# Attention backward: fewer tiles of dS turned on TensorE, more dP tiles on GpSimd, and smaller pieces of the turned QKV weights

## The chip, the core and the metric

The kernel runs on one core of a Trainium2 chip. A core has five engines that work side by side and meet at semaphores: PE (TensorE, matrix products into PSUM), DVE (VectorE), ACT (ScalarE), POOL (GpSimd) and SP (SyncE, which here only issues DMAs). Sixteen DMA engines move the data. The metric is the device time of one launch in microseconds (us); lower is better. The kernel before takes 2510.57 us, the median of three runs (2510.35 to 2513.57).

## The reference

The program computes the output of one transformer block and the gradients of ten of its inputs. The sequence has S = 2048 rows of D = 512 values, there are 32 heads of width 16, and the MLP is 1792 wide. Cut to what matters:

```python
mod = (silu(c) @ w_mod).reshape(1, 6, 1, 512)      # sa, ca, ga, sb, cb, gb
h = layernorm(x) * (1 + ca) + sa
q, k, v = heads(h @ wqkv)                          # 32 heads, Dh = 16
p = softmax(q @ k.T * Dh ** -0.5)
x = x + ga * (merge(p @ v) @ wo)
h = layernorm(x) * (1 + cb) + sb
x = x + gb * (relu(h @ w1 + b1) ** 2 @ w2 + b2)
out, vjp = jax.vjp(block, x, wqkv, wo, w1, b1, w2, b2, c, w_mod)
return out, *vjp(grad_out)
```

The change lies in the backward of the softmax attention. For each head it needs the scores again, P = exp(scale q k^T) (the row sums have been worked into dO and the delta term before), dP = dO v^T - delta, dS = P * dP, and from these dV = P^T dO, dK = dS^T q and dQ = dS k.

## The kernel before, in words

The program is one chain of stages. From the start to about 980 us runs the attention forward, with the QKV projection and the MLP forward as filler; from there to about 1168 us the MLP backward; from about 1168 to 2385 us the attention backward (`attn_bwd`, L1431 on), which is what the change touches; and to 2509 us the weight gradients of QKV and `wo`, the input gradient and the modulation (`phase6`).

**Tiling of the attention backward.** The outer loops run over eight head groups `g` of four heads, and over two pairs `jp` of heads in each: 16 pairs in all. In a pair, `c` runs over four chunks of 512 query columns, and `ib0` over four **groups** of four key-side blocks of 128 rows. So a pair has 16 groups; the text numbers them m = 0 to 15 (L1586). A group is even or odd by m. A group has four steps `i`, a step has the two heads `a` of the pair.

**A step.** For each head PE makes a score tile `st` (L1601, 128x512 in PSUM) and, one step behind, the `dp` tile of the step before (L1522). These two use different halves of the array's rows. ACT takes `st` to `pu = exp(st)` (L1604). DVE takes `dp` and `pu` to `ds = dp * pu` (L1526, bf16 in SBUF). PSUM holds three `st` tiles (pool `p5st`) and three `dp` tiles (`p5dp`), so PE can be at most that far ahead of ACT and of DVE. PE also runs `kv` (L1459, four small matmuls side by side for dK and dV of a step, `kv_two`), and `dq` (L1484, four matmuls side by side for dQ).

**Turning dS.** `dq` needs dS transposed. The `ds` of a whole group (32 blocks of 128x128) is turned by one DMA on SP's queue (`dS`, L1543) into one of five buffers `dsT` (the fifth is a part of `keep`). In the even groups PE turns the four blocks of the first step's first head itself (`turn_ds`, L1550: four transposes at L1559 into a tile from the `st` pool, and one copy by ACT at L1560), so that group's DMA turns only 28 blocks. In the odd groups the DMA turns all 32. Two consecutive groups are put together: their eight `dq` calls are queued (`pendq`) when the second one's DMA is issued, and PE starts them two groups later, two calls in step 0 and two in step 2 of each group (L1614). The text calls two such groups, an even one and the odd one behind it, a **window**.

**Help from GpSimd.** In the odd groups (`off`, L1528), one of the eight dS tiles, that of step 1 and head 1, isn't made by DVE: ACT copies the `dp` tile to SBUF (`dP_pool`, L1534, into `junk6` or `csq` in turn) and POOL multiplies (L1535). In the odd groups the `kv` work is also spread differently: one step's `kv` after the first head and one at the end of the step, in place of two at the end.

**Loads.** The next pair's and next group's operands come in pieces: before each group POOL issues the piece that is due (L1586 to L1590), after a one-element copy `tick` (L1589) that reads a recent `ds` and so holds the issue back to its place. The pieces of a pair are evenly spaced over its 16 groups: 16 in most. In the first pair of the last head group (g = 7, jp = 0) there are 16 as well: four of `pair_pieces`, four of the QKV weights and eight of `WmT`, the turned QKV weights that `phase6` needs (`load_wmt`, 128 rows of 1536 bytes each). All engines keep the order in which the program is written here; nothing is reordered by a scheduler in this stage.

Every so often there is more: at the end of a chunk ACT takes dK and dV out of PSUM (`kvT`, L1462, four in a pair), and in groups 2, 3 and 7 of a pair the finished dK, dV and dQ of the pair before are turned on PE (`turn`, L1472 and L1500) and copied by ACT (L1476, L1502).

The lines that order it, from the functions printed below:

```python
        def off(c, ib):
            return (c * SC + ib // G) % 2 == 1
...
                            if i == 2:
                                turn_ds(dsg, grp, off(c, ib), end and m > 2)
```

Of the kernel before, what the change touches and what calls it, by code (L numbers as in the profile page):

```python
# [19 lines left out]
P = 128  # L20
# [15 lines left out]
class Background:  # L36
# [13 lines left out]
    def next(self):  # L50
        while self.gens:
            r = next(self.gens[0], None)
            if r is not None:
                if isinstance(r, tuple):
                    self.mark = r[0]
                    self.seen.add(r[0])
                return r
            self.gens.pop(0)
        return None
# [46 lines left out]
class K:  # L106
# [1277 lines left out]
    def load_wmt(self):  # L1384

        D, DT = self.D, self.DT
        self.WmT = self.wp.tile([P, DT, 3 * DT, P], BF16, name="WmT")
        return [(self.WmT[:, kt, n:n + 6].rearrange("p n k -> p (n k)"), self.WmT_d[kt, :, n * P:(n + 6) * P])
                for kt in range(DT) for n in range(0, 3 * DT, 6)]

    def load_group(self, g):

# [4 lines left out]
        if g < 2:  # L1397
            T, o = {}, 0
            for n, e in width.items():
                if g:  # L1400
                    T[n] = qp.tile([P, e], BF16, name=f"{n}g")[:]
                elif n == "K":
                    T[n] = self.keep[:, :e]
                else:
                    T[n] = self.q0[:, o:o + e]
                    o += e
            self.Tq[g] = T
        T, pieces = self.Tq[g % 2], []
        for n, (src, rows) in fm.items():
# [21 lines left out]
    def attn_bwd(self):  # L1431
# [8 lines left out]
        S, D, H, NQ, ST, SC = self.S, self.D, self.H, self.NQ, self.ST, self.SC  # L1440
        G = 4
# [8 lines left out]
        pend, pendq, turnq, two = [], [], [], []  # L1450
        own = dT_free[-1]

        def kv(u):
            (T, g, jp, c, ib, kvT, pu, ds) = u
            for j, (n, src) in enumerate((("Q", ds), ("dO", pu))):
                for a in range(2):
                    r = 64 * j + 32 * a
                    col = (2 * jp + a) * DH
                    nc.tensor.matmul(acckv[r:r + DH, :], lhsT=T[n][:, ib, col:col + DH], rhs=src[:, a, :],  # L1459
                                     start=(ib == 0), stop=(ib == ST - 1))  # L1460
            if ib == ST - 1:
                nc.scalar.activation(kvT[:, 512 * c:512 * (c + 1)], acckv[:], ACT.Copy, scale=kvs[:])  # L1462
# [42 lines left out]
        def kv_two(n=2):  # L1505
            for _ in range(n):
                u = pend.pop(0)
                kv(u)
                (T, g, jp, c, ib, kvT, pu, ds) = u
                if ib < ST - 1:  # L1510
                    continue
                if c % 2 and (g, jp) == (NQ - 1, 1):
                    turnq.append((g, jp, kvT, 4 * (c - 1)))
                elif c == SC - 1:
                    turnq.extend((g, jp, kvT, s0) for s0 in (0, ST // 2))

        def dP(u, a):

            (T, g, jp, c, ib, kvT, pu, dsg, i, grp) = u
            rd = slice(64 - 64 * jp, 128 - 64 * jp)  # L1520
            dp = dpp.tile([P, 512], F32, name="dp")
            nc.tensor.matmul(dp[:], lhsT=T["dOT"][rd, ib * P:(ib + 1) * P],  # L1522
                             rhs=masked["VT"][a][rd, 512 * c:512 * (c + 1)], start=True, stop=True)
            if a == 1 and i == 1 and off(c, ib):
                return dp
            nc.vector.tensor_tensor(dsg[:, i, a], dp[:], pu[:, a, :], ALU.mult)  # L1526

        def off(c, ib):  # L1528
            return (c * SC + ib // G) % 2 == 1

        def dP_pool(u, dp):
            (T, g, jp, c, ib, kvT, pu, dsg, i, grp) = u
            f = (self.junk6, self.csq)[(c * SC + ib // G) // 2 % 2]
            nc.scalar.copy(f[:], dp[:])  # L1534
            nc.gpsimd.tensor_tensor(dsg[:, i, 1], f[:], pu[:, 1, :], ALU.mult)  # L1535

# [13 lines left out]
        def turn_ds(dsg, grp, skip, late):  # L1550

            dsT = next(t for t in dT_free if not late or t is not own)
            dT_free[:] = [t for t in dT_free if t is not dsT]
            grp.extend((dsT, 0 if skip else 4))
            if skip:
                return
            tp = stp.tile([P, 4, P], BF16, name="st")
            for b in range(4):
                nc.tensor.transpose(tp[:, b, :], dsg[:, 0, 0, b * P:(b + 1) * P], self.ident[:])  # L1559
            nc.scalar.copy(dsT[:, 0:4 * P], tp[:].rearrange("p b k -> p (b k)"))  # L1560

        tick = self.tick
        T = self.T0
        last = None
        for g in range(NQ):
            for jp in range(2):
                if jp == 0:
                    if g + 1 < NQ:
                        Tn, later = self.load_group(g + 1)
                    else:  # L1570
                        Tn, later = None, self.wq_pieces(1) + self.load_wmt()
                    cut = len(later) // 2 if Tn else len(later)
                    pieces = self.pair_pieces(g, 1) + later[:cut]
                    later = later[cut:]
                elif g + 1 < NQ:
                    pieces = self.pair_pieces(g + 1, 0) + later
                else:
                    pieces = [(self.xhat1_6[:, st, :], self.xhat1_d.rearrange("(st p) d -> p st d", p=P)[:, st, :])
                              for st in range(ST)]
                kvT = kvp.tile([P, S], BF16, name="kvT")  # L1580
                end = (g, jp) == (NQ - 1, 1)
                total = len(pieces)
                for c in range(SC):
                    c0 = 512 * c
                    for ib0 in range(0, ST, G):
                        m = c * (ST // G) + ib0 // G  # L1586
                        while pieces and (total - len(pieces)) * SC * ST <= m * G * total:
                            if last:
                                nc.gpsimd.tensor_copy(tick[:], last[7][0:1, 0, 0, 0:1])  # L1589
                            nc.gpsimd.dma_start(*pieces.pop(0))  # L1590
                        dsg, grp = self.dsp.tile([P, G, 2, 512], BF16, name="ds"), []
                        for i in range(G):
                            ib = ib0 + i
                            q = slice(ib * P, (ib + 1) * P)
                            if turnq and i == 3 and m >= (7 if turnq[0][2] is None else 2):
                                turn(*turnq.pop(0))
                            pu = self.pup.tile([P, 2, 512], BF16, name="pu")
                            for a in range(2):
                                stt = stp.tile([P, 512], F32, name="st")
                                rs = slice(64 * jp, 64 * jp + 64)  # L1600
                                nc.tensor.matmul(stt[:], lhsT=T["QT"][rs, q], rhs=masked["KT"][a][rs, c0:c0 + 512],  # L1601
                                                 start=True, stop=True)
                                held = dP(last, a) if last else None
                                nc.scalar.activation(pu[:, a, :], stt[:], ACT.Exp, scale=self.scale)  # L1604
                                if held is not None:
                                    dP_pool(last, held)
                                if a == 0 and i % 2 == 1 and off(c, ib) and len(pend) >= 4:
                                    kv_two(1)
                            if last:
                                dS(last)  # L1610
                            last = (T, g, jp, c, ib, kvT, pu, dsg, i, grp)
                            if i % 2 == 1 and len(pend) >= 4:
                                kv_two(1 if off(c, ib) else 2)
                            elif i % 2 == 0 and len(pendq) > 2 * G:  # L1614
                                for _ in range(4 if end else 2):
                                    dq(pendq.pop(0))
                            if i == 2:
                                turn_ds(dsg, grp, off(c, ib), end and m > 2)
            T = Tn
        with tc.manual_schedule(engines=ALL):  # L1620
            for t in (2, 0):
# [337 lines left out]
```

## Time and profile before

| what | value |
|---|---|
| median of 3 runs | 2510.57 us (2510.35 to 2513.57) |
| the profiled execution's own time | 2511.14 us |
| its span, first to last instruction | 2509.0 us |
| mean granted TensorE clock | 0.997 of full speed |
| attention backward in the span | about 1168 to 2385 us |
| exps of it (L1604) | 2048, 128 in a pair of heads |
| dS tiles by DVE (L1526) / by POOL (L1535) | 1920 / 128 |
| transposes of dS by PE (L1559) / copies of them by ACT (L1560) | 512 / 128 |
| DMA transposes (L1543) | 256, half of 28 blocks and half of 32 |

The span is what the profile covers; the device time is 2.1 us longer, for what lies around it. A row of the profile names a line, an engine, an operation and the tiles it writes and reads (out<-in), then the number of instructions, the busy time and the mean length of one. The length of one is longer than its share of the time where instructions overlap in the engine's pipeline: what counts for the pace is the distance from one start to the next. A view of the time line merges instructions of the same kind that follow each other: start, length of the whole stretch, and their number behind an x.

### The profile page before, as it was taken

The page shows a single profiled execution, that of the slowest core. Times are in us where ns is not written, and L with a number is a line of the kernel's source. Part 1 is how long each engine was busy: PE and PEld are TensorE (multiplying, and loading weights), DVE is VectorE, ACT ScalarE, POOL GpSimd, SP SyncE. Part 2 cuts the span into 40 slices and gives each one's busy share as a digit, 9 for nine tenths or more (in the row PEclk, how much of TensorE's full clock was granted, in tenths as well). Part 3 has the DMA queues.
Part 4 walks back from the last instruction along what each step waited for, and adds up shares of the span by engine and source line. Part 5 has one row for each costly group of instructions (what it writes and reads, how often), then busy time and mean ns, then how long its engine had stood idle before and what let it go on. Part 6 is the DMA issues. An engine that isn't in the chain of part 4 may idle for free.

```text
span 2509.0 us, 68721 instructions
## 1 busy us (share of the span) xinstructions
PE 2438.6 (97%) x26695; PEld 1080.0 (43%) x26695; DVE 1709.6 (68%) x3519; ACT 2295.0 (91%) x3789; POOL 716.4 (29%) x1289
## 2 busy tenths in 40 slices
PE   8999999999999999999999999999999999999998
PEld 4555555555555554573333333333333333333343
DVE  6222322422332344677999999999999999999957
ACT  7999999999999997534999999999999999999935
POOL 2344531220131022245222222222222222222223
PEclk9999999999999999999999999999999999999999
DMA  4688661441243044598999999999999999999997
GB/s 166 133 180 208 170 121 50 129 100 39 99 115 90 23 131 138 122 199 214 236 215 227 224 221 228 223 222 221 229 222 222 230 223 222 225 226 232 233 191 208
DMA packets 1260526, 445.78 MB, mean 178 GB/s; under 512 B 1204052, under 2 KB 1228246, under 8 KB 1260198
## 3 DMA queue, kind: packets, MB, share of 16 engines
q1 hardware_dynamic: 1219654, 336.29, 70.7%
q0 software_dynamic: 38464, 104.04, 13.6%
q8 instruction: 209, 3.42, 0.6%
q10 hardware_dynamic: 2080, 1.05, 0.1%
q14 instruction: 119, 0.97, 0.1%
HBM read 75.83 MB, written 64.49 MB: 56 GB/s over the span
## 4 chain that ended last, share of the span: by engine, by line
PE 58%; ACT 27%; DMA 7%; issue 4%; DVE 3%; POOL 1%; SPq 0%; DVEq 0%; ACTq 0%; POOLq 0%
ACT pu L391 18%; PE st L1601 17%; PE acckv L1459 8%; PE st L388 8%; ACT pu L1604 7%; PE accq L1484 5%; DMA dsT<-ds 3%; PE accbank L322 3%; PE dps L1050 2%; PE pps L1237 2%; PE st L1559 1%; PE dp L1522 1%; PE dp L1652 1%; DVE ds L1526 1%; DMA keep<-ds 1%
## 5 line engine op out<-in xcount | busy, mean ns | idle before, releaser
L1526 DVE TENSOR_TENSOR ds<-dp,pu 128x512 bf16<-128x512 f32 x1920 | 1181.7, 684 | 25.1 <-PE dp L1522 19.1
L1604 ACT ACTIVATE pu<-st 128x512 bf16<-128x512 f32 x2048 | 1072.7, 661 | 30.1 <-PE st L1601 21.3
L391 ACT ACTIVATE pu<-st 128x1024 bf16<-128x1024 f32 x992 | 912.2, 1077 | 5.1 <-PE st L388 4.9
L388 PE MATMUL st<-QTm,KTq 128*128 128x512 bf16 x1984 | 588.4, 377 | 20.0 <-ACT pu L391 6.0
L322 PEld LDWEIGHTS <-pu 128*128 128x128 bf16 x8192 | 347.3, 96 | 236.3 <-issue 3.2
L1522 PE MATMUL dp<-kvm,q 64*128 64x512 bf16 x1024 | 364.1, 384 | 1.5 <-DVE ds L1526 0.7
L1522 PE MATMUL dp<-kvm,dOTg 64*128 64x512 bf16 x1024 | 361.8, 384 | 0.5 <-DVE ds L1526 0.4
L322 PE MATMUL accbank<-Vaug,pu 128*128 128x17 bf16 x8192 | 357.7, 171 | 1.2 <-ACT Vaug L522 0.9
L1601 PE MATMUL st<-kvm,q 64*128 64x512 bf16 x1024 | 351.6, 381 | 6.0 <-ACT pu L1604 0.2
L1601 PE MATMUL st<-kvm,QTg 64*128 64x512 bf16 x1024 | 350.6, 381 | 6.8
L388 PEld LDWEIGHTS <-KTq 128*128 128x128 bf16 x1984 | 188.2, 96 | 177.5 <-issue 125.6
L1535 POOL TENSOR_TENSOR ds<-junk,pu 128x512 bf16<-128x512 f32 x64 | 73.8, 1153 | 372.2 <-ACT junk L1534 302.4
L1459 PE MATMUL acckv<-ds,Qg 128*16 128x512 bf16 x1024 | 176.0, 382 | 0.2
L1459 PE MATMUL acckv<-pu,dOg 128*16 128x512 bf16 x1024 | 175.9, 382 | 0.0
L1459 PE MATMUL acckv<-ds,q 128*16 128x512 bf16 x1024 | 175.8, 382 | 0.0
L1459 PE MATMUL acckv<-pu,q 128*16 128x512 bf16 x1024 | 175.8, 382 | 0.0
L1535 POOL TENSOR_TENSOR ds<-csq,pu 128x512 bf16<-128x512 f32 x64 | 73.8, 1154 | 349.6 <-ACT csq L1534 271.5
L302 POOL DMA_DIRECT2D QTm<-QTq_d x124 | 63.8, 516 | 341.5 <-PE st L388 319.9
L1601 PEld LDWEIGHTS <-q 64*128 64x128 bf16 x1024 | 66.9, 94 | 159.6 <-issue 144.0
L1601 PEld LDWEIGHTS <-QTg 64*128 64x128 bf16 x1024 | 67.0, 94 | 158.2 <-issue 141.3
L329 DVE RECIPROCAL rl<-accbank 128x4 f32<-128x4 f32 x128 | 23.0, 179 | 159.0 <-PE accbank L322 158.8
L1522 PEld LDWEIGHTS <-q 64*128 64x128 bf16 x1024 | 89.8, 93 | 56.7 <-issue 50.4
(390 smaller groups left out, 3197.0 us busy)
## 6 DMA issues: line engine op xcount, KB each, us to landing
KTq<-KTq_d POOLq DMA_DIRECT2D x24, 512.0 KB, 3.8
duT_d<-auT POOLq DMA_DIRECT2D x3, 1792.0 KB, 7.6
aT_d<-rT POOLq DMA_DIRECT2D x3, 1792.0 KB, 11.0
KTq_d<-KTq SPq DMA_DIRECT2D x32, 128.0 KB, 2.1
QTq_d<-ev_fm SPq DMA_DIRECT2D x32, 128.0 KB, 4.3
ktm_d<-ev_tm POOLq DMA_DIRECT2D x32, 128.0 KB, 2.5
VTq_d<-vT POOLq DMA_DIRECT2D x4, 1024.0 KB, 6.2
dx<-dx_d SPq DMA_DIRECT2D x16, 256.0 KB, 5.3
```

Source lines behind the costliest of these rows:

```text
L302: nc.gpsimd.dma_start(QTm[j][32 * j:32 * j + 32, :], self.QTq_d[g, 32 * j:32 * j + 32, 512 * qc:512 * (qc + 1)])
L322: nc.tensor.matmul(acc[:, a, sub, :], lhsT=pu[:, a, sub * P:(sub + 1) * P], rhs=Vaug[:, kb, h, :], start=(kb == 0 and a == 0 and sub == 0) ...
L388: nc.tensor.matmul(stt[:, a, :], lhsT=KT[:, kb * P:(kb + 1) * P], rhs=QTm[2 * jp + a][:], start=True, stop=True)
L391: nc.scalar.activation(pu[:], stt[:], ACT.Exp, scale=self.scale)
L1050: nc.tensor.matmul(pt[:], lhsT=a[st], rhs=g_tm[:, st, :], start=(st == 0), stop=(st == ST - 1))
L1459: nc.tensor.matmul(acckv[r:r + DH, :], lhsT=T[n][:, ib, col:col + DH], rhs=src[:, a, :], start=(ib == 0), stop=(ib == ST - 1))
L1484: nc.tensor.matmul(accq[r:r + 32, o:o + 256], lhsT=T["K"][:, 4 * c + sub, col:col + 32], rhs=v[:, r // 32 % 2 * 2:r // 32 % 2 * 2 + 2, 4 * ...
L1522: nc.tensor.matmul(dp[:], lhsT=T["dOT"][rd, ib * P:(ib + 1) * P], rhs=masked["VT"][a][rd, 512 * c:512 * (c + 1)], start=True, stop=True)
L1526: nc.vector.tensor_tensor(dsg[:, i, a], dp[:], pu[:, a, :], ALU.mult)
L1535: nc.gpsimd.tensor_tensor(dsg[:, i, 1], f[:], pu[:, 1, :], ALU.mult)
L1601: nc.tensor.matmul(stt[:], lhsT=T["QT"][rs, q], rhs=masked["KT"][a][rs, c0:c0 + 512], start=True, stop=True)
L1604: nc.scalar.activation(pu[:, a, :], stt[:], ACT.Exp, scale=self.scale)
```

## The change

It has three parts. First, `turn_ds` is called with another rule, `no_turn`: PE turns its four blocks only in groups 0, 4, 8 and 12 of a pair. In groups 2, 6, 10 and 14 the transposes on PE and ACT's copy are gone, and the DMA turns 32 blocks there. Second, `off` is also true in groups 10 and 14, so that ten tiles of a pair go by ACT and POOL in place of eight; the rule for spreading `kv` keeps the old condition under the name `odd`. `dP_pool` takes `csq` in odd groups and `junk6` in even ones. Third, `WmT` is fetched in sixteen pieces of 128 rows of 768 bytes in place of eight of 1536 bytes, one in each of the first 14 pairs as the fifth piece of the pair (behind the four of `pair_pieces`), and two in the 15th, which is the first of the last head group and then has ten pieces in place of 16. Most pairs then have 17 pieces, and a new clause issues what is left before group 15.

```diff
-        return [(self.WmT[:, kt, n:n + 6].rearrange("p n k -> p (n k)"), self.WmT_d[kt, :, n * P:(n + 6) * P])
-                for kt in range(DT) for n in range(0, 3 * DT, 6)]
+        return [(self.WmT[:, kt, n:n + 3].rearrange("p n k -> p (n k)"), self.WmT_d[kt, :, n * P:(n + 3) * P])
+                for kt in range(DT) for n in range(0, 3 * DT, 3)]
...
+        def odd(c, ib):
+            return (c * SC + ib // G) % 2 == 1
+
+        def no_turn(c, ib):
+            return ib // G > 0
+
         def off(c, ib):
-            return (c * SC + ib // G) % 2 == 1
+            return odd(c, ib) or (c > 1 and ib // G == 2)
 
         def dP_pool(u, dp):
             (T, g, jp, c, ib, kvT, pu, dsg, i, grp) = u
-            f = (self.junk6, self.csq)[(c * SC + ib // G) // 2 % 2]
+            f = (self.junk6, self.csq)[(c * SC + ib // G) % 2]
...
+        wmt = self.load_wmt()
...
-                        Tn, later = None, self.wq_pieces(1) + self.load_wmt()
+                        Tn, later = None, self.wq_pieces(1) + wmt[2 * g + 1:]
                     cut = len(later) // 2 if Tn else len(later)
-                    pieces = self.pair_pieces(g, 1) + later[:cut]
-                    later = later[cut:]
+                    pieces = self.pair_pieces(g, 1) + wmt[2 * g:2 * g + 1] + later[:cut]
+                    later = wmt[2 * g + 1:2 * g + 2] + later[cut:]
...
-                        while pieces and (total - len(pieces)) * SC * ST <= m * G * total:
+                        while pieces and ((total - len(pieces)) * SC * ST <= m * G * total or m == SC * ST // G - 1):
...
-                                if a == 0 and i % 2 == 1 and off(c, ib) and len(pend) >= 4:
+                                if a == 0 and i % 2 == 1 and odd(c, ib) and len(pend) >= 4:
                                     kv_two(1)
...
-                                kv_two(1 if off(c, ib) else 2)
+                                kv_two(1 if odd(c, ib) else 2)
...
-                                turn_ds(dsg, grp, off(c, ib), end and m > 2)
+                                turn_ds(dsg, grp, no_turn(c, ib), end and m > 2)
```

## The prediction

> **What bounds the kernel now.** First the page's head: shares of busy time, then the span in 40 slices of 62.7 us.
>
> ```profile
> PE 2438.6 (97%) x26695; PEld 1080.0 (43%) x26695; DVE 1709.6 (68%) x3519; ACT 2295.0 (91%) x3789; POOL 716.4 (29%) x1289
> ...
> DVE  6222322422332344677999999999999999999957
> ACT  7999999999999997534999999999999999999935
> ...
> DMA  4688661441243044598999999999999999999997
> ```
>
> The attention backward is slices 19 to 38. There DVE and ACT are at nine tenths or more together with the DMA row, so the page names no single bound, and PE's digit says little, since ends of matmuls are modelled. So I read one pair of heads in detail, first in the chain of waits, from 1880 to 1930 us:
>
> ```profile
> by line: PE st L1601 37.7%; PE acckv L1459 17.5%; DMA keep<-ds 17.0%; ACT pu L1604 14.3%; PE accq L1484 10.6%; issue 3.7%; PE st L1559 3.3%; PE dp L1522 2.8%; ACT junk L1534 1.9%; ACT dq_t L1502 1.4%; ACT dsT L1560 0.8%; ACT kvT L1462 0.6%;
> ...
> 1908.33 0.54 PE acckv L1459 x8
> 1909.53 0.33 PE accq L1484 x8
> 1909.86 0.33 PE st L1559 x4
> ...
> 1927.16 8.52 DMA keep<-ds
> ```
>
> PE carries most of this chain, with DMA landings (17.0%) and ACT's exps (14.3%). The three lines in the middle are an even group: two kv (0.54), two dq (0.33), then the four transposes of dS (0.33 us), all on the path. The last is a wait for a landing of 8.52 us. Next, ACT's time line:
>
> ```profile
> 1896.67 0.73 ACT L1534 COPY junk<-dp 128x512 f32<-128x512 f32 x1
> 1897.13 4.20 ACT L1604 ACTIVATE pu<-st 128x512 bf16<-128x512 f32 x8
> 1901.19 0.62 ACT L1560 COPY keep<-st 128x512 bf16<-128x512 bf16 x1
> 1901.66 4.26 ACT L1604 ACTIVATE pu<-st 128x512 bf16<-128x512 f32 x8
> 1905.80 0.59 ACT L1534 COPY csq<-dp 128x512 f32<-128x512 f32 x1
> ```
>
> L1560 and L1534 stand at the same place of a group (behind the sixth exp), so from one to the next is one group's length: group 9 at 1896.67, 10 at 1901.19, 11 at 1905.80. The window of groups 10 and 11 takes 9.13 us. From the other copies of this view (1858.18, 1867.93; 1877.75, 1886.86; 1905.80, 1915.11; 1924.19) the window (2,3) takes 9.75, (6,7) 9.11, (12,13) 9.31 and (14,15) 9.08 us; the pair takes 75.6.
>
> What each engine asks for in a window: back to back, exps start every 0.477 us (the closest starts in the trace), a copy takes 0.47 (1905.80 to the exp at 1906.27), a copy of a turned dK or dV 0.27, kvT 0.57. ACT: 16 exps and two copies, 16 x 0.477 + 2 x 0.47 = **8.57**, plus 0.53 in groups 2, 3 and 7 and 0.57 at each chunk. DVE's start to start is (4.28 - 0.68) / 6 = **0.60**:
>
> ```profile
> 1863.71 4.28 DVE L1526 TENSOR_TENSOR ds<-dp,pu 128x512 bf16<-128x512 f32 x7 [0.20 <-PE dp L1522]
> ```
>
> 15 tiles in a window are 9.0 us. So (10,11) and (14,15) are DVE's plus 0.1; (6,7) too; (2,3) is nobody's alone: ACT asks for 9.1, DVE 9.0, and the chain shows PE in between. With three PSUM tiles an engine can't save idle time up over more than one or two tiles, so a saving counts only in the group where that engine is last.
>
> **Part one: four turns of a pair leave PE and ACT.** PE loses 64 x 0.33 = 21.1 us, ACT 64 x 0.47 = 30 us, over 16 pairs, in groups 2, 6, 10 and 14; and a tile of the st pool is free there for scores. In (2,3) ACT falls to 8.6, DVE stays at 9.0, and PE's 0.33 comes off the chain: I take 0.33 a pair (ends: 0, were DVE alone the bound, and 0.47). In (6,7) DVE's 9.0 stays, 9.11 can lose only **0.1**.
>
> The price is on SP and the DMAs: four more blocks in 64 transposes.
>
> ```profile
> L1543 SPq DMA_TRANSPOSE dsT<-ds x208: 3399/4099/6260, 1174.8 to 2385.4; - x104
> ```
>
> Split by group in the trace, a DMA of 28 blocks holds SP 3.78 us (median) and one of 32 blocks 4.22: **0.44 us for four blocks**, 64 x 0.44 = 28 us. SP's issues take 8 x (3.78 + 4.22) = 64.0 of the pair's 75.6 us, later 65.8. SP is free before 103 of the 128 odd groups' DMAs for over 0.15 us, so its own queue hides the 0.44. Here the Trainium skill speaks against the change: "VectorE: DVE Perf Modes", sections "The three transpose paths" and "Rules for kernel authors", gives 390 ns for a 128x128 transpose on TensorE and 1309 ns on the DMA's path, and advises TensorE where PSUM will do as the destination. By its figures four blocks would cost the queue 5.2 us and save PE 1.56; 64 x 5.2 = 335 us doesn't fit into 16 x 11.6 = 186 us of SP's free time, and the kernel would lose some 150 us. The trace's rows are 0.44 and 0.33 for the same four blocks[...]. I take the rows.
>
> **Part two: two more tiles of a pair by ACT and POOL.** In groups 10 and 14 DVE drops to 7 tiles, 14 x 0.60 = 8.4 us in the window; ACT gets a copy (0.47) for the one it loses and stays at 8.57. ACT is then last. With the same 0.13 over the bound as today, (10,11) goes from 9.13 to 8.70 and (14,15) from 9.08 to 8.70: **0.43 + 0.38**. POOL's two products (1.15 us each) lie in its idle time (29% busy), and kv asks for the tile three steps (over 3 us) later; without that cover each would cost kv 1.15. `csq` is then written every 9 us and read within 2. The Trainium skill's "SBUF — State Buffer", section "SBUF: two separate sides", has GpSimd and DVE share a port pair as an exclusive lock. If it bound here, 32 products would take 32 x 1.15 = 37 us of DVE's time for the 32 x 0.60 = 19 they give it. The row of this case:
>
> ```profile
> L1526 DVE TENSOR_TENSOR ds<-dp,pu x1920: 680/681/694, 1169.9 to 2384.6; 128x512 bf16<-128x512 f32 x192
> ...
> L1535 POOL TENSOR_TENSOR ds<-junk,pu x64: 1145/1153/1163, 1177.0 to 2374.1; 128x512 bf16<-128x512 f32 x64
> ```
>
> The longest of 1920 DVE tiles is 13 ns over the median, with 128 products beside them. No block; I charge nothing.
>
> **The wait that is nearest.** A window's dq starts two groups after its second DMA is issued.
>
> ```profile
> PE accq L1484 <- DMA dsT<-ds: 6.3, 9, 2.5
> ```
>
> The view counts 9 waits over 150 ns; by starts in the trace, the dq that needs the odd group's blocks comes within 0.12 us of the landing in 29 of 128 windows, together 12.6 us of PE's time, with a quarter of the windows under 0.17 us of slack and the median at 0.67. The odd group's DMA lands 7.66 us (median) after its issue. The window between that issue and dq is (2,3), (10,11) or (14,15) for three dq sets of a pair, and these get 0.3 to 0.4 shorter: of 48, some 40% have less slack than that and lose about 0.3 each, 48 x 0.4 x 0.3 = **6 us** back. Between 0 (PE's lead over ACT hides it) and 15 (all of them held by the full 0.3). Behind the held dq stand the next scores, so ACT and DVE wait too.
>
> **Part three: WmT.** Eight pieces leave the 15th pair, which took 78.1 us against about 75.6 for most; sixteen half ones come, one in each of the first 14 pairs and two in the 15th, each with a tick (0.18) and an issue (0.56) on idle POOL. I take 1.5 of the 2.5 us for it. A row of 768 bytes beside the 512-byte pieces that pass today costs the other pairs little: between 0 and 0.3 us a pair (one landing more that is late), I take none; the last pieces at group 15 are used over two groups later.
>
> **Sum.** A pair gains 0.33 + 0.1 + 0.43 + 0.38 = 1.24; 16 pairs 19.8; less 6 for dq, plus 1.5: **15.3 us**. The profiled execution goes from 2511.1 (span 2509.0 and 2.1 around it) to 2495.8; it lies 0.6 over the median, so I forecast **2495 us**. The ends: 2480, all of 64 x 0.47 = 30 us, were ACT the bound in every one of these groups; 2507, DVE's 19 us alone, less 15 for dq. That the change doesn't do what it says is excluded by the instruction streams: PE has 256 transposes fewer, POOL 32 products more.
>
> **Rivals.**
> - *The landing decides, slower.* If four more blocks delay the odd group's landing not by their 0.44 on SP, but by the whole distance between the two kinds (6.57 against 7.66, so 1.1 us), the dq sets behind groups 2, 6, 10 and 14 are late: with median slacks of 0.91, 0.73, 0.73 and 0.04, 0.2 + 0.4 + 0.4 + 1.05 = 2.0 us a pair, 32 in all: **2527**. It decides from about 0.75 us on, where it eats the 15. For it: chain lines of 8.5 us landings. Against: odd DMAs issued right behind another (gap below 0.15) land after 7.82, with gaps over 0.8 after 7.53.
> - *Nothing.* The shorter windows run into the landings, so every window's gain above 0.2 goes back; what stays is part three and (6,7): **2508**. For it: 29 held windows already. Against: the median slack is 0.67.
> - *More.* ACT's 8.57 binds without the 0.13, and (2,3) gives 0.47: 4.5 more, **2490**; it lies in the forecast's own range.
>
> **Chances.** Forecast with *More* 0.68, *Nothing* 0.17, *Slower* 0.15. Under 0.2%, 5 us, this kernel's measurement can't tell a change from none: faster 0.70 (some of *Nothing* ends beyond 5), same 0.15, slower 0.15. The likeliest case's own range is 2480 to 2505; to leave out no more than two in ten it goes up to 2518.
>
> **What would show it.** Copies at groups 10 and 14 read L1534's name, with 8.7 us windows; L1559's count is 256; DVE loses some 19 us busy; SP's 32-block issues stay near 4.2. Wrong, if windows (10,11) stay at 9.1 with PE's waits for dsT grown beyond 30 us, if DVE tiles reach 1 us, or if odd landings pass 8.4.

## The result and the profile after

The changed kernel takes 2506.34 us, the median of 21 runs (2500.32 to 2511.66), beside 2509.84 us for the kernel before (21 runs, 2502.70 to 2516.53): ratio 0.9983, 95% interval [0.9975, 0.9991]. So it is faster, by 2 to 6 us, some 4; the forecast was 15. The profiled execution is the fastest of the 21, with a span of 2498.5 us and a clock of 0.998, so its distance to the span of before (10.5 us) isn't the change's: of these, 6.3 us lie in the attention backward (1215.2 to 1208.9 us from the first exp to the start of the last group), the rest in stages that the change doesn't touch.

First the page's head and slices again (busy time of each engine; below, tenths of 40 slices):

```profile
PE 2410.2 (96%) x26211; PEld 1061.6 (42%) x26439; DVE 1695.0 (68%) x3487; ACT 2283.1 (91%) x3757; POOL 753.5 (30%) x1337
...
DVE  6222322422332343576999999999999999999957
ACT  7999999999999997534999999999999999999945
...
DMA  4589661541243045499999999999999999999997
```

DVE has 1695.0 us in place of 1709.6, ACT 2283.1 in place of 2295.0; every row of the backward stays at nine tenths. POOL goes from 716 to 753. The chain of waits, of the same stretch of the same pair as before (1879 to 1929 us), summed by line:

```profile
by line: PE st L1608 38.5%; PE acckv L1459 18.5%; ACT pu L1611 16.2%; PE accq L1484 11.3%; issue 4.8%; PE dp L1522 4.3%; PE st L1565 2.0%; ACT csq L1540 1.9%; ACT kvT L1462 1.7%; ACT dsT L1566 1.5%; PE st L1500 0.7%
```

The four transposes' share goes from 3.3% to 2.0%: they are gone from every second even group. This stretch held no wait for a landing, where one took 17.0% before; without it all other shares grow by a fifth, so the exps' rise from 14.3 to 16.2% says nothing of the change. ACT's time line, groups 9 to 11 of the 14th pair (start, length of the stretch, operation):

```profile
2194.75 0.74 ACT L1540 COPY csq<-dp 128x512 f32<-128x512 f32 x1
2195.21 4.21 ACT L1611 ACTIVATE pu<-st 128x512 bf16<-128x512 f32 x8
2199.28 0.62 ACT L1540 COPY junk<-dp 128x512 f32<-128x512 f32 x1
2199.74 4.16 ACT L1611 ACTIVATE pu<-st 128x512 bf16<-128x512 f32 x8
2203.79 0.59 ACT L1540 COPY csq<-dp 128x512 f32<-128x512 f32 x1
```

All three copies are now L1540, copies of dp tiles: group 10 gives a tile to POOL. From copy to copy group 10 takes 4.53 us and group 11 takes 4.51. The window is **9.04** us where 9.13 was read before and 8.70 was forecast. The other rows that were shown of before:

```profile
L1526 DVE TENSOR_TENSOR ds<-dp,pu x1888: 677/680/693, 1168.5 to 2376.9; 128x512 bf16<-128x512 f32 x189
...
L1541 POOL TENSOR_TENSOR ds<-csq,pu x128: 1142/1149/1160, 1175.6 to 2375.7; 128x512 bf16<-128x512 f32 x128
```

DVE has 32 tiles fewer and its longest is 693 ns beside a median of 680, with 160 products on POOL: no lock. Issues of the transposing DMAs on SP (least, median and greatest ns of one), and PE's waits for their landings (us in total, times, longest):

```profile
L1549 SPq DMA_TRANSPOSE dsT<-ds x208: 3490/4262/6457, 1173.4 to 2377.8; - x104
```

```profile
PE accq L1484 <- DMA dsT<-ds: 8.5, 13, 2.9
```

SP's median issue rises from 4.10 to 4.26 us. With `keep` counted, SP is busy 70.0 us of a pair, 66.7 before (sums over the trace). And it runs back to back more often: an odd group's DMA starts within 0.15 us of the end of the one before it 54 times of 128, 25 times before.

**Two measures.** Pairs of heads repeat so exactly that a group's start-to-start length has a floor that most pairs hit. I take for each of the 16 groups the value that a fifth of the pairs are under, and call their sum the *undisturbed pair*; the *excess* is what the 16 pairs of a profile take over that. A dq set counts as *held* when its start lies within 0.12 us of the landing it needs. All three come from starts and landings in the traces, one profiled execution of each kernel; that execution can lie some us from the median in the first column.

| kernel | median us | ratio to before | undisturbed pair | excess, 16 pairs | held sets of 128 | SP busy of a pair |
|---|---|---|---|---|---|---|
| before | 2509.84 | | 75.33 | 10 | 29 | 66.7 |
| changed | 2506.34 | 0.9983 | 74.55 | 17 | 31 | 70.0 |
| part one alone | 2515.87 | 1.0024 | 74.90 | 18 | 37 | 70.2 |
| part two alone | 2522.01 | 1.0041 | 75.92 | 9 | 22 | 66.5 |
| part three alone | 2509.48 | 0.9998 | 75.33 | 10 | 25 | 66.6 |
| before, DMA of 32 in groups 2, 6, 10, 14 | 2520.51 | 1.0036 | 75.40 | 14 | 41 | 70.2 |
| before, halved DMA | 2499.84 | 0.9954 | 75.36 | 2 | 0 | 32.0 |
| changed, halved DMA | 2490.99 | 0.9914 | 74.57 | 4 | 0 | 34.9 |
| part one and three, halved DMA | 2491.21 | 0.9930 | 74.89 | 3 | 0 | |
| the same without ACT's copy and DVE's tile | 2480.37 | 0.9886 | 74.02 | 5 | 0 | |

The undisturbed pair loses 0.78 us, 12.5 over 16 pairs; the excess takes some 6 back. Which part does which is what the runs were for.

### The profile page after: what moved, and what is told of

Same layout as the page of the kernel before. It is cut to its first block, busy times and chain, and to the rows that moved or that the text cites. A ratio compares the mean times of both kernels' runs of the same rounds, so it can differ in the third digit from the quotient of the medians.

```text
span 2498.5 us, 67897 instructions
## 1 busy us (share of the span) xinstructions
PE 2410.2 (96%) x26211; PEld 1061.6 (42%) x26439; DVE 1695.0 (68%) x3487; ACT 2283.1 (91%) x3757; POOL 753.5 (30%) x1337
## 4 chain that ended last, share of the span: by engine, by line
PE 49%; ACT 35%; DMA 7%; issue 5%; DVE 3%; POOL 1%; SPq 1%; ACTq 0%; DVEq 0%; POOLq 0%
ACT pu L391 26%; PE st L1608 17%; PE acckv L1459 8%; ACT pu L1611 6%; DMA dsT<-ds 5%; PE accq L1484 5%; PE st L388 4%; PE dp L1522 2%; PE accbank L322 2%; PE dps L1050 2%; PE dp L1659 1%; PE st L1754 1%; ACT csq L1540 1%; PE pps L1237 1%; DVE ds L1526 1%
## 5 line engine op out<-in xcount | busy, mean ns | idle before, releaser
L1526 DVE TENSOR_TENSOR ds<-dp,pu 128x512 bf16<-128x512 f32 x1888 | 1166.0, 682 | 34.6 <-PE dp L1522 19.1
L388 PE MATMUL st<-QTm,KTq 128*128 128x512 bf16 x1859 | 560.9, 377 | 27.1 <-ACT pu L391 6.1
L1541 POOL TENSOR_TENSOR ds<-csq,pu 128x512 bf16<-128x512 f32 x128 | 147.2, 1150 | 627.0 <-ACT csq L1540 553.6
L1522 PEld LDWEIGHTS <-dOTg 64*128 64x128 bf16 x1024 | 88.2, 93 | 52.9 <-issue 43.8
```

The costliest lines, as they stand in the source:

```text
L388: nc.tensor.matmul(stt[:, a, :], lhsT=KT[:, kb * P:(kb + 1) * P], rhs=QTm[2 * jp + a][:], start=True, stop=True)
```

## The experiments

**One part at a time.** Part one alone: `turn_ds` in the kernel before with the new rule, nothing else.

```diff
-                                turn_ds(dsg, grp, off(c, ib), end and m > 2)
+                                turn_ds(dsg, grp, ib // G > 0, end and m > 2)
```

> Part one alone: four turns of a pair instead of eight, eight tiles by POOL, WmT in eight pieces at the end. Theory L (three score tiles keep PE's lead over ACT short, so groups 10 and 14 are paced by PE's blocks between scores and ACT, not by DVE): DVE's tile more in groups 10 and 14 costs nothing, windows (10,11) and (14,15) stay within 0.1 us of the changed kernel's 9.04, and the kernel comes out 2 to 8 us below before, like the whole change. Theory D (DVE bounds these windows, the prediction's): windows (10,11) and (14,15) stay at 9.1, only (2,3) and (6,7) shrink, and the time is 4 us below before or less, with the undisturbed pair at 75.0 or more.

It is slower: 2515.87 us, ratio 1.0024 [1.0008, 1.0041]. The undisturbed pair falls by 0.43 us, 6.9 us over 16 pairs, and the excess rises by some 8 (10 to 18), so that in the profiles the backward is 0.7 us longer than before. The profiled execution took 2510.38 us; where the median's other 5 us arise, it can't show. ACT's copies around groups 10 and 11 of the 14th pair:

```profile
2198.04 0.73 ACT L1534 COPY junk<-dp 128x512 f32<-128x512 f32 x1
2207.09 0.59 ACT L1534 COPY csq<-dp 128x512 f32<-128x512 f32 x1
```

From one to the other are 9.05 us. By the floors over all pairs group 10 takes 4.34 and 11 takes 4.68, so the window is 9.02 with DVE's tile kept, just over DVE's 9.0: both theories' numbers for the windows are near (9.04 and 9.1), and neither foresaw a slower kernel.

Part two alone: `off` with groups 10 and 14, turns as before.

> Part two alone: ten tiles by ACT and POOL, PE still turns in all eight even groups. Theory L: groups 10 and 14 now carry ACT's copy of the dP tile on top of the copy of the turned blocks (two copies of 0.47), so they grow from 4.57 to about 4.9 or 5.0 us and the kernel is 8 to 15 us slower. Theory D: DVE's relief is worth 0.4 a window against ACT's 0.47 more, so (10,11) stays near 9.1 and the time is that of before within 4 us.

Slower by 10 us, ratio 1.0041 [1.0026, 1.0057]. ACT's time line of groups 9 to 11 in the 14th pair:

```profile
2204.18 0.73 ACT L1537 COPY csq<-dp 128x512 f32<-128x512 f32 x1
...
2208.70 0.62 ACT L1537 COPY junk<-dp 128x512 f32<-128x512 f32 x1
2209.16 0.64 ACT L1563 COPY dsT<-st 128x512 bf16<-128x512 bf16 x1
...
2213.70 0.59 ACT L1537 COPY csq<-dp 128x512 f32<-128x512 f32 x1
```

Between the copies at 2204.18 and 2213.70 lie 9.52 us: group 10 carries two copies, one of the dp tile and one of the turned blocks, and is 5.0 us long. The undisturbed pair grows by 0.59 us, 9.4 over 16 pairs, which is the whole loss. L's numbers hold; only part one frees the place on ACT that part two uses.

Part three alone: the sixteen pieces of `WmT`.

> Part three alone. Prediction: the 15th pair falls from 78.1 to about 75.6 us, the others stay, 1.5 to 2.5 us below before. Theory W (the extra pieces in every pair make landings of transposes late): the 15th pair gains the same, but windows with a held dq rise from 29 to 40 or more and the time is that of before or up to 4 us above.

Ratio 0.9998 [0.9984, 1.0012]. The 15th pair takes 75.95 us in place of 78.11, but in this profile the eighth takes 78.07, which took 75.86 before. What it gives is inside the noise, and held sets don't rise.

**What holds groups 10 and 14.** The changed kernel, with kv spread in groups 2, 6, 10 and 14 as in odd groups:

```diff
+        def spread(c, ib):
+            return odd(c, ib) or ib // G == 2
+
...
-                                if a == 0 and i % 2 == 1 and odd(c, ib) and len(pend) >= 4:
+                                if a == 0 and i % 2 == 1 and spread(c, ib) and len(pend) >= 4:
...
-                                kv_two(1 if odd(c, ib) else 2)
+                                kv_two(1 if spread(c, ib) else 2)
```

> The changed kernel with one edit more: in groups 2, 6, 10 and 14 kv is spread as in odd groups (one step's kv after the first head, one at the end) in place of two at the end. Theory L: the block of 0.84 us between two scores goes there, ACT's gaps behind it go, windows (10,11) and (14,15) fall from 9.04 to 8.6 to 8.8 us, and an undisturbed pair from 74.6 to about 73.8. Theory D says DVE is last: no change in the windows. The time then tells how much of a shorter pair the landings take back: 2 to 10 us below the changed kernel if little, the same as it if all.

The windows went up, from 9.04 to 9.12 (group 10 4.63, 11 4.49), the undisturbed pair to 74.91, the time to 2512.26 us, ratio 1.0009 [0.9991, 1.0026]. So spreading the two kv doesn't shorten these windows: theory L falls in the form I gave it.

**The price of four blocks.** The kernel before, with DMAs of 32 blocks in groups 2, 6, 10 and 14 although PE turns its four there too:

```diff
-            grp.extend((dsT, 0 if skip else 4))
+            grp.extend((dsT, 0 if skip or more else 4))
...
-                                turn_ds(dsg, grp, off(c, ib), end and m > 2)
+                                turn_ds(dsg, grp, off(c, ib), end and m > 2, ib // G > 0)
```

> The kernel before, with the suspected price alone: in groups 2, 6, 10 and 14 the DMA turns all 32 blocks although PE turns its four as well (the same values land twice). PE, ACT and DVE do what they did. Theory G (the landings take the gain back): the sum of what groups take over their undisturbed length rises from about 10 us to 16 or more, and the time is 5 to 12 us over before. Theory N (four blocks are hidden on SP): within 2 us of before.

Ratio 1.0036 [1.0023, 1.0048], **6 to 12 us slower** for the blocks alone, with the undisturbed pair as before. SP's issues and who waited for them (the last line is us in total and times):

```profile
L1543 SPq DMA_TRANSPOSE dsT<-ds x208: 3395/4234/6457, 1174.7 to 2389.6; - x104
...
  PE accq L1484: 9.5, 15
```

The median issue is 4.23 us, PE's waits over 150 ns are 15 in place of 11, and held sets 41 in place of 29; odd groups' DMAs that start within 0.15 us of the one before are 57 in place of 25. This is the price, with the work of the engines unchanged. The excess rose only from 10 to 14, less than the 16 that theory G asked for: the time followed G, this profile only in part.

**Later dq.** If only the held dq were behind it, more time for a landing would end it: no dq in step 0 of an even group, then three, three and two.

```diff
-                                for _ in range(4 if end else 2):
+                                for _ in range(4 if end else (0, 3, 3, 2)[m % 2 * 2 + i // 2]):
```

> The kernel before with dq started half a group later: none in step 0 of an even group, three in step 2, three in step 0 and two in step 2 of the odd one, in place of two everywhere; the same work, the same buffers, and some 2.3 us more for a landing. Theory G: no dq is held by a landing (29 of 128 windows now), the excess over undisturbed groups falls from 10 us to under 5, and the time is 5 to 8 us below before. Theory N: the excess has another cause and stays near 10; the time stays within 3 us.

> The changed kernel with the same later dq. Theory G: the excess falls from 17 us to under 5, and the kernel now shows the gain of its shorter windows: 10 to 15 us below the kernel before with the later dq, so some 2491 us. Theory N: the same distance to the kernel before with later dq as without, 3 to 4 us.

Held sets fall to 3 in both. But the times go up, to 2516.14 (1.0020 [1.0010, 1.0029]) and 2516.76 us (1.0032 [1.0015, 1.0049]), and the excess of the second stays at 17. The undisturbed pair costs 0.4 and 0.56 us more in this order, 6 and 9 us. And the wait has moved. PE's and DVE's waits in the changed kernel with later dq:

```profile
PE accq L1484 <- DMA dsT<-ds: 1.1, 2, 0.9
```

```profile
DVE ds L1526 <- DMA dsT<-ds: 3.7, 6, 1.0
...
DVE ds L1526 <- DMA keep<-ds: 0.8, 2, 0.6
```

A `ds` tile is one of three buffers, so DVE's first write of a group needs the landing of three groups before. The profiles of before and of the changed kernel show no DVE wait for a landing in this stage (the view lists those over 150 ns); here there are eight. Two consumers stand behind the same landings, and relieving one brings up the other. Theory G's mechanism was named too narrowly. In the kernel before with later dq there is one such wait (2.1 us), and the 0.4 us a pair of the new order account for its loss.

**Halving the DMA.** The DMA turns blocks up to the 16th only, and dq reads those twice; the blocks left out are missing from dQ.

```diff
-                nc.sync.dma_start_transpose(dsT.rearrange("p (b k) -> p b k", k=P)[:, n:, :],
-                                            dsg[:].rearrange("p i a k -> p (i a k)")[:, n * P:])
+                nc.sync.dma_start_transpose(dsT.rearrange("p (b k) -> p b k", k=P)[:, n:16, :],
+                                            dsg[:].rearrange("p i a k -> p (i a k)")[:, n * P:16 * P])
...
-                                 rhs=v[:, r // 32 % 2 * 2:r // 32 % 2 * 2 + 2, 4 * a + sub, :],
+                                 rhs=v[:, 0:2, 4 * a + sub, :],
```

> The kernel before with the DMA turning only the first 16 blocks of a group (12 where PE turns four); dq reads those blocks twice, so dQ isn't the reference's, and PE, ACT, DVE and POOL do the same work. SP's issues fall from 66.7 to about 33 us of a pair. Theory S (SP's issues are near full, a late one holds dq or the ds buffers): the excess over undisturbed groups falls from 10 us to under 5, the time 5 us or more below before. Theory X (the excess has another source): it stays.

> The changed kernel with the same halved DMA (it leaves out the same blocks). Theory S: the excess falls from 17 us to under 5 and the whole gain on undisturbed groups is seen, 12 to 16 us below the kernel before with halved DMA. Theory X: the distance stays at 3 to 4 us.

The edit does two things: a landing comes sooner after its issue, and the issue itself can come sooner, as the DMA reads only the first two steps' tiles. In the halved kernels an even group's DMA is issued about 1 us before the next group's first exp, in the whole ones over 1 us behind it.

Both runs shared a chip: 2499.84 us (0.9954 [0.9940, 0.9968]) and 2490.99 (0.9914 [0.9902, 0.9926]). In the second, an issue on SP and its landing:

```profile
L1549 SPq DMA_TRANSPOSE dsT<-ds x208: 1392/2203/4052, 1174.6 to 2368.1; - x104
...
DMA to landing us min/median/max: 3.2/4.4/7.1
```

No dq is held, the excess is 2 and 4 us, and the undisturbed pairs are those of the whole kernels to 0.03 us. With landings out of the way the change is worth 8.9 us (2499.84 less 2490.99; 10 by the ratios, 10.6 in the backward of the two profiles), with them 3.5. With five and six runs the 10 carry some 5 us each way, so it is the excess (2 and 4 in place of 10 and 17) that makes the reading firm. Landings cost the kernel before about 10 us and the changed one about 15. As the edit shortens the DMA and advances it, these runs don't tell SP's time from the DMA's own. The 12 to 16 that I had written for theory S was too much.

**Two tries at a better version.** The group's DMA cut in two, three steps' blocks a step earlier and the last step's 8 behind them:

> The changed kernel with each group's DMA cut in two, three steps' blocks issued one step earlier and the last step's 8 blocks at the old place; the whole computation. The last landing comes about 1 us earlier if SP's time goes by blocks alone. Theory S: the excess falls from 17 us towards 8, the time 5 to 9 us below the changed kernel. If each DMA has a fixed price of some 0.5 us or more, SP overflows (32 issues a pair) and the time is above the changed kernel.

It takes 2586.49 us, ratio 1.0305 [1.0285, 1.0325]. Issues, and who waited for them:

```profile
L1550 SPq DMA_TRANSPOSE dsT<-ds x416: 1232/2184/10036, 1173.1 to 2462.2; - x139
...
  PE accq L1484: 50.3, 68
  DVE ds L1526: 31.5, 25
```

The shortest issue, of 8 blocks, is 1.23 us; by blocks alone it would be 3.97 / 4 = 1.0 (the least issue of 32 in groups 1 and 3 of before is 3.97), so cutting a DMA in two costs SP time. SP is now busy 77.4 us of a pair (sum over the trace), more than the 74.56 of an undisturbed pair: it can't keep up.

The other: kv in even steps and dq in odd ones, so that a landing may come one step later.

> The kernel before with the places of kv and dq exchanged: kv in steps 0 and 2, dq in steps 1 and 3, the turns on PE one step later, and POOL's tile that of step 0. The same work, and a landing may come one step (1.1 us) later before it holds dq. Theory S: held dq sets fall from 29 of 128 to under 8 and the excess from 10 us to 5, the time 3 to 6 us below before, if the undisturbed pair stays at 75.3; each tenth of a microsecond that the new order costs a pair adds 1.6.

> The changed kernel with the same exchange. Theory S: held dq sets fall from 31 to under 8 and the excess from 17 us to about 10 (the ds buffers still wait for landings, as with the later dq), the time 4 to 8 us below the changed kernel, some 2500, if the undisturbed pair stays at 74.55.

Held sets fall to 7 and 8, but the undisturbed pair becomes 80.02 and 78.65 us, and the times 2578.05 (1.0268 [1.0249, 1.0287]) and 2564.74 us (1.0197 [1.0176, 1.0219]). PE's longest wait:

```profile
PE acckv L1459 <- ACT kvT L1462: 49.2, 63, 0.8
```

The first kv of a chunk now meets ACT's `kvT` of the chunk before, a wait that the kernel before doesn't show. No version that I tried beats the changed kernel and computes all.

**What part two pays.** The changed kernel without part two, with halved DMA:

> The changed kernel without part two (eight tiles by POOL), with the halved DMA of the two earlier runs (blocks left out in the same way), so that landings don't blur it. Against the changed kernel with halved DMA it tells what part two alone is worth. Theory D (the prediction's 0.81 us a pair): 13 us slower, 2504. Theory E (DVE's tile was last only in part, as the undisturbed groups of the two unhalved runs say, 0.35 a pair): 5 to 6 us slower, 2496 to 2497.

And in that kernel, groups 10 and 14 without DVE's tile and without ACT's copy (POOL's product of `pu` with itself stands in for that dS tile):

> The run above with DVE's tile of groups 10 and 14 taken away at no price to ACT: POOL multiplies pu by itself for it, so that this dS tile isn't the product, and dp isn't copied (the DMA halved as above). ACT asks for 8.1 us in windows (10,11) and (14,15), DVE for 8.4. Theory D: DVE binds and these windows fall from 9.0 to 8.5. Theory P (PE's own order and the hand-over of tiles bind there): they stay within 0.15 us of 9.0. In between: ACT's copy is what part two pays with, and windows of 8.6 to 8.8 show it.

Without part two 2491.21 us (0.9930 [0.9916, 0.9944]), 0.2 us from the changed kernel with halved DMA by the medians and 4 by the two ratios, which are the fairer measure, as the two ran on different chips; the interval of that 4 reaches from about nothing to 8. The undisturbed pair is 0.32 longer. With the tile gone at no price 2480.37 (0.9886 [0.9869, 0.9902]). Its ACT time line, groups 9 to 11 of the 14th pair:

```profile
2177.69 0.73 ACT L1543 COPY csq<-dp 128x512 f32<-128x512 f32 x1
2178.16 8.29 ACT L1614 ACTIVATE pu<-st 128x512 bf16<-128x512 f32 x16
2186.34 0.59 ACT L1543 COPY csq<-dp 128x512 f32<-128x512 f32 x1
```

From 2177.69 to 2186.34 are 8.65 us, with 16 exps and one copy: the window falls by 0.39 when DVE's tile goes and ACT gets nothing for it, and by nothing (9.03 to 9.04) when ACT gets its copy of 0.47. So ACT's copy eats what DVE's tile gives. One thing stays mixed in: in this run nothing reads that `dp` tile, so PE gets its buffer back without waiting for a reader.

Last, four score tiles and two dp tiles in PSUM, with halved DMA (the last weight-gradient sum of the tail is then kept in a score tile):

> The changed kernel with halved DMA, four score tiles and two dp tiles in PSUM in place of three and three (and one weight-gradient sum of the tail in a score tile). Theory L (PE's lead over ACT is what three score tiles allow): ACT's gaps go, an undisturbed pair falls from 74.57 to below 74.0, 8 us or more. If two dp tiles are too few for DVE, the pair grows instead, by more than 1 us: then PE's lead over DVE binds as much, and L isn't told apart further.

2686.60 us, ratio 1.0711 [1.0692, 1.0731], the undisturbed pair 86.46, and DVE's first wait:

```profile
DVE ds L1526 <- PE dp L1522: 85.2, 216, 0.9
```

Two dp tiles are far too few, so this doesn't tell whether a fourth score tile would help.

## Why the prediction was wrong

**Part one: right.** Forecast 0.33 + 0.1 = 0.43 us a pair; part one alone takes 0.43 off the undisturbed pair (75.33 to 74.90). The number is right in part by luck: by the groups' floors (2,3) loses 0.38, (6,7) 0.14 and, against the forecast, (10,11) and (14,15) 0.11 each, while groups 0, 4 and 12, which turn as before, take 0.11 longer each. What the sum left out cancels.

**Part two: the step that failed.** The text said "ACT is then last. With the same 0.13 over the bound as today, (10,11) goes from 9.13 to 8.70". Forecast 0.81 a pair, 13.0 us. Measured on top of part one: 0.35 a pair (74.90 to 74.55), 5.6 us, and 0.2 to 4 us in the halved runs. The gain is in the groups behind (group 0 5.34 to 5.10, group 12 5.12 to 4.95), and the windows themselves gain nothing: (10,11) goes from 9.02 to 9.04, (14,15) from 8.97 to 9.03. The 0.13 (9.13 less 9.0) was what a window took over *DVE's* demand. Over ACT's demand the same window took 0.56 already, and I put DVE's small allowance on ACT's number. In the changed kernel it takes 9.04 - 8.57 = 0.47 over ACT. The chain of waits of the changed kernel shows where such time lies:

```profile
2194.27 0.74 ACT pu L1611
2195.01 0.48 ACT csq L1540
2195.49 0.51 ACT pu L1611
...
2197.09 0.31 PE st L1608
...
2197.42 0.54 PE acckv L1459 x8
2197.95 0.32 PE st L1608
...
2198.28 0.21 PE st L1608
...
2198.49 0.33 PE accq L1484 x8
```

Up to 2196 it runs through ACT's exps and copy, then it stays on PE: a score (0.31), two kv (0.54), the next scores (0.32 and 0.21), two dq (0.33). The exp at 2198.31 in this stretch starts 0.69 behind the one before, in place of 0.48, and 0.42 behind its score. ACT pays for PE's blocks although it has work for only 8.57, and PE pays for ACT's copies: neither is full. How much of the 0.47 is PE's order and how much the three tiles each way is open; spreading kv didn't take it away.

**DVE as the bound.** It was right that DVE's tile counted (0.39 a window, when it goes for nothing), and wrong that its relief could be had for one copy on ACT. "ACT gets a copy (0.47) for the one it loses" compared ACT with the kernel before, but part one had already made that place free. The runs say that the two have to be had together: with the place free and DVE's tile kept the window is 9.03, with the tile gone and the place filled 9.04, with both free 8.65.

**The landings: size about right, mechanism too small.** I took 6 us (0 to 15). The four blocks alone cost 9 (6 to 12), and the halved runs put what landings take of this change at 8.9 - 3.5 = 5.4 us. But I had set aside SP's own queue ("its own queue hides the 0.44") by medians, 64.0 to 65.8 us of a pair. That step failed too. SP's real load is 66.7 to 70.0 of some 75, and the DMAs of odd groups that start right behind another went from 25 of 128 to 54 (55 with part one alone, 57 with the blocks alone, 16 with part two alone): SP doesn't hide the four blocks, it passes them on. And the second consumer, the three `ds` buffers, wasn't in the sum.

**Part three.** Forecast 1.5 us; measured 0.5, between 4 us faster and 3 slower: no gain shown.

**Rules and rows.** The decision for the rows held. Four blocks more on a DMA cost SP 0.44 us, not 5.2; but they cost 9 us at the end, so for part one by itself, which made the kernel slower, the advice of the Trainium skill's "VectorE: DVE Perf Modes", section "Rules for kernel authors", to transpose on TensorE pointed the right way here; its figures had made it 150. GpSimd and DVE didn't block each other (693 ns at most beside a median of 680). The Trainium skill's "SBUF — State Buffer", section "SBUF: two separate sides", which the prediction held against part two, has DVE take the lock in a two-port mode or with two inputs in SBUF, and `ds` has one input in PSUM; no run here tries the other case.

**Sum by the runs.** 12.5 us from the undisturbed pairs, less 5 to 9 for the landings, nothing for part three: 3.5 to 7.5, measured 2 to 6. Of the rivals, *Nothing* was nearest (2508), with half of its mechanism: landings did take a part back, but part two's windows never got shorter, and part three and (6,7) are not what stayed. The forecast's range of 2480 to 2518 holds the time, its size is off by a factor of four.

**Open.** Part one alone lies 6 us above before and the whole 4 below; parts two and three then give some 10 us together in full kernels, but 0.2 to 4 in the halved ones and 5.6 by the undisturbed pairs. Held sets are fewer with part two (31 against 37), which may be the rest; the intervals of the runs are some 4 us wide, which may be it as well. No run tells.

## What to carry to other kernels

An allowance over a bound belongs to the engine it was measured on: when a change makes another engine last, take the time over *that* engine's demand from the same window, not the small one of the old bound. Where two engines are within a few per cent of each other, moving work off one at a price on the other should be counted at the price. And a queue that is busy 88% of a repeating period, as SP was here (66.7 of 75.6 us), has little reserve: add up its issues with means, and list every consumer of its landings, the buffers that wait to be written as well as the reader.

## What the runs showed of the hardware

A transposing DMA held SP's queue, at the least, for 3.40 us with 28 blocks, for 3.94 with 32, for 1.39 with 12 (the halved runs) and for 1.23 with 8 (the cut one): it grows with the blocks, and 8 cost more than a quarter of 32. Halving the blocks brought the median landing from 7.2 to 4.4 us after the issue.

A late landing was also followed by a lower clock of PE. In the first pair of the changed kernel PE waited 2.9 us for one landing. The view by stretches there (us; then busy time of PE, PEld, DVE, ACT and POOL with counts, the granted clock, the share of the DMAs, GB/s):

```profile
1213.00:1217.00 4.00, 1.20 (x10) 0.30 (x7) 2.02 (x4) 2.12 (x5) 1.79 (x3) 1.00 1.12 101
1217.00:1222.00 5.00, 4.78 (x42) 0.85 (x41) 2.78 (x5) 3.50 (x7) 0.77 (x1) 0.66 1.30 219
1222.00:1230.00 8.00, 8.00 (x94) 2.52 (x91) 7.88 (x14) 7.70 (x17) 3.54 (x8) 1.00 1.12 260
```

In the stretch after the wait the granted clock is 0.66, and score matmuls take 0.60 to 0.63 us there in place of 0.37 to 0.39; that group took 8.6 us in place of 4.5. One wait of 2.9 us so cost 4.1. It was not the only case: with kv spread, PE waited up to 3.5 us in the first pair, and the clock was 0.50 and 0.53 in the two stretches of 2 us behind it. That the wait brings the lower clock is read from this order of events; no run varied it.
